# Linear attention and a top-1 expert layer on one core: PSUM banks apart, casts moved, key turns left out, late tiles routed singly, 112 partitions

## The chip, the core and the metric

The kernel runs on one core of a Trainium2 chip. A core has five engines with queues of their own: TensorE (PE, with its weight loads as PEld) multiplies matrices into PSUM, VectorE (DVE), ScalarE (ACT) and GpSimd (POOL) work on elements, and SyncE (SP) issues most transfers. Each queue runs in order; engines wait for each other by semaphores. The kernel uses PSUM as eight banks of 512 float32 values per partition. The metric is the device time in microseconds: 324.94 us before (median of three runs, 324.41 to 328.82).

## The reference

```python
for t in range(S):                                  # q, k, v, alpha: (B 4, H 8, S 768, D 48), float32
    state = alpha[:, :, t, :, None] * state + np.einsum('bhd,bhe->bhde', k[:, :, t], v[:, :, t])
    y[:, :, t] = np.einsum('bhd,bhde->bhe', q[:, :, t], state)
x = y.transpose(0, 2, 1, 3).reshape(3072, 384)
do = x @ w_skip > 0                                 # rows not chosen stay as they are
logits = x[do] @ w_gate                             # 8 experts
e_idx = argmax(logits); gate = softmax(logits)[e_idx]
out[do] = x[do] + gate * (relu(x[do] @ w1[e_idx]) @ w2[e_idx])    # w1: 384x1024, w2: 1024x384 per expert
```

## The kernel before

**Attention.** The 3072 rows are 24 tiles of 128 time steps (`NT`), all eight heads of one batch each; `G` = 2 batches alternate, six chunks (`C`) each. On partitions, keys, queries and decays (one buffer `qka`, loaded in three transfers) hold two heads of 48 features in rows 0 to 47 and 64 to 111; four such pairs (`NP`) lie side by side. Rows 48 to 63 and 112 to 127 are zeros. Per tile: two scans with the decays (`pfx`, `sfx`, L232, L240) and the products that scale queries and keys (L236, L242), three tiles ahead; scores into `ps_s` (L257), masked into `st` by VectorE (L266) and ScalarE (L272); the turned keys `kt` (`turn_k`, L280, L282) for the state update (`outer`, L293); the outputs into `ps_y` in two halves (L313). Between the halves `fence` makes ScalarE write one element, `spot` (L344), because both halves write the same bank. Then `turn_y`, and `rows` (L359) with the logits of the router.

**Routing.** `route` finds each row's expert (`m`), `rank` counts rows per expert with two matmuls, `place` makes slot numbers, `one_hot` and `marks` (`mv`) build the table that says which rows expert e gathers (L458). The steps of a group are handed out between the attention steps by `tick`. Tiles 18 to 23 come last; their rows for expert 0 are not fetched from memory but multiplied straight into place (`late_rows`, with the one-hot `mine`), and expert 0's other rows are fetched early (`early_rows`).

**Experts.** For each expert, four first-layer sets `up` of 18 products (L629) fill a bank of `ps_h` with two 240-column halves; ScalarE evicts `hh` (L633) and VectorE the rest `hl` (L634). Two second-layer passes `down` of 24 products (L645) follow; between them `turn` transposes the next expert's gathered rows in two halves through `ps_x` (L609, evicted at L611, L612). Weights are split into a high part on ScalarE and a low part on VectorE or GpSimd (L556, L560), a few pieces after each set. `guard` reads all decays and checks their range on ScalarE (`over`, L597) in experts 0 to 4. Both kinds of bank come from attention's tiles:

```python
self.ps = pp.tile([P, 2, 512], F32, name="ps_s")          # two banks, one tile
self.py = pp.tile([P, 2, 512], F32, name="ps_y")
self.ps_x = bank((self.ps[:, 0, :], self.ps[:, 1, :]), DM)
self.ps_h = bank((self.py[:, 0, :], self.py[:, 1, :], self.pg), 2 * ROOM)
```

The order on each engine is that of the program text; waits are put in by the framework, which follows PSUM accesses by tile.

## Time and profile before

| | |
|---|---|
| median of three runs | 324.94 us |
| the profiled execution: time, span | 327.61 us, 325.9 us |
| PE, PEld busy | 270.8 us (83%), 250.9 us (77%) |
| DVE, ACT, POOL busy | 198.2 us (61%), 159.5 us (49%), 179.2 us (55%) |
| transfers | 65.30 MB, mean 200 GB/s |
| attention, from the first scores to the last tile's rows | 7.8 to 136 us |
| experts, from the first set to the last pass | 143.9 to 319.3 us |

The span runs from the first to the last instruction; 1.7 us lie outside it. Busy shares are means over stages with different limits, so a change in one stage has to be read in that stage: which wait ends last there, and what then comes next. [...]

### The profile page before, as it was taken

The page shows a single profiled execution, that of the slowest core. Times are in us where ns is not written, and L with a number is a line of the kernel's source. Part 1 is how long each engine was busy: PE and PEld are TensorE (multiplying, and loading weights), DVE is VectorE, ACT ScalarE, POOL GpSimd, SP SyncE. Part 2 cuts the span into 40 slices and gives each one's busy share as a digit, 9 for nine tenths or more (in the row PEclk, how much of TensorE's full clock was granted, in tenths as well). Part 3 has the DMA queues.
Part 4 walks back from the last instruction along what each step waited for, and adds up shares of the span by engine and source line. Part 5 has one row for each costly group of instructions (what it writes and reads, how often), then busy time and mean ns, then how long its engine had stood idle before and what let it go on. Part 6 is the DMA issues. An engine that isn't in the chain of part 4 may idle for free.

```text
span 325.9 us, 9204 instructions
## 1 busy us (share of the span) xinstructions
PE 270.8 (83%) x3766; PEld 250.9 (77%) x3766; DVE 198.2 (61%) x362; ACT 159.5 (49%) x338; POOL 179.2 (55%) x199
## 2 busy tenths in 40 slices
PE   0798999898889799893989886878897888898891
PEld 0687987787778688683989886878887888898791
DVE  5765788778778886574555534535438456563720
ACT  3144554545456545612447385495495554453500
POOL 4545564648778978761574552643736265542611
PEclk9998999889999979996799997997999999999998
DMA  7987688969888964713372539449259557250001
GB/s 255 353 309 227 189 271 294 299 209 330 286 250 258 318 202 148 246 54 109 114 251 70 211 90 392 144 162 394 84 186 350 193 171 251 65 195 26 10 12 34
DMA packets 32178, 65.30 MB, mean 200 GB/s; under 512 B 4469, under 2 KB 11535, under 8 KB 32128
## 3 DMA queue, kind: packets, MB, share of 16 engines
q1 hardware_dynamic: 29952, 59.59, 54.9%
q0 software_dynamic: 2176, 5.05, 4.8%
q8 instruction: 31, 0.51, 0.6%
q14 instruction: 19, 0.16, 0.2%
HBM read 56.99 MB, written 8.85 MB: 202 GB/s over the span
## 4 chain that ended last, share of the span: by engine, by line
PE 59%; DVE 13%; ACT 8%; POOL 7%; issue 7%; DMA 3%; SPq 1%; POOLq 0%; DVEq 0%; ACTq 0%
PE ps_y L629 12%; PE ps_c L645 10%; PE ps_y L313 7%; PE ps_v L645 6%; PE ps_g L629 5%; PE ps_s L257 5%; PE ps_g L359 3%; PE ps_k L280 3%; ACT over L597 3%; DVE sfx L240 2%; PE ps_v L458 2%; PE ps_v L293 2%; ACT w1h L556 2%; PE ps_s L609 2%; DVE hl L634 2%
## 5 line engine op out<-in xcount | busy, mean ns | idle before, releaser
L257 PE MATMUL ps_s<-qka 64*64 64x128 f32 (+1 forms) x768 | 33.5, 270 | 11.1 <-DVE qka L242 7.8
L313 PE MATMUL ps_y<-st,vt 64*48 64x128 f32 (+1 forms) x768 | 36.7, 260 | 6.6 <-ACT spot L344 6.1
L560 POOL TENSOR_TENSOR w1l<-raw,w1h 128x512 fp32r<-128x512 f32 x24 | 31.3, 1305 | 17.0 <-ACT w1h L556 13.5
L629 PE MATMUL ps_y<-xh,w1h 128*128 128x240 f32 x132 | 25.3, 300 | 17.1 <-DVE hl L634 16.8
L242 POOL TENSOR_TENSOR qka<-qka,sfx 128x512 f32<-128x512 f32 x23 | 29.4, 1279 | 17.6 <-DVE sfx L240 12.8
L236 POOL TENSOR_TENSOR qka<-qka,pfx 128x512 f32<-128x512 f32 x24 | 26.3, 1095 | 21.1 <-DVE pfx L232 7.9
L651 POOL DMA_INDIRECT out_dram<-o,ids x16 | 17.6, 1098 | 36.9 <-DVE o L649 31.7
L257 PEld LDWEIGHTS ps_s<-qka 64*64 64x64 f32 x768 | 27.0, 143 | 12.4 <-POOL st L160 7.8
L560 POOL TENSOR_TENSOR w2l<-raw,w2h 128x512 fp32r<-128x512 f32 x16 | 21.2, 1327 | 27.1 <-ACT w2h L556 25.9
L629 PEld LDWEIGHTS ps_y<-xh,w1h 128*128 128x128 f32 x132 | 20.4, 205 | 18.8 <-DVE hl L634 18.4
L313 PEld LDWEIGHTS ps_y<-st,vt 64*48 64x48 f32 x768 | 26.8, 129 | 8.9 <-ACT spot L344 7.1
L272 ACT COPY st<-ps_s 64x512 f32<-64x512 f32 x24 | 13.9, 579 | 36.8 <-DVE st L266 30.4
L633 ACT ACTIVATE hh<-ps_y 128x480 fp32r<-128x480 f32 x22 | 12.5, 570 | 38.9 <-PE ps_y L629 35.7
L634 DVE SCALAR_TENSOR_TENSOR hl<-ps_y,hh 128x480 fp32r<-128x480 f32 x22 | 14.4, 652 | 28.1 <-ACT hh L633 28.1
L560 DVE TENSOR_TENSOR w2l<-raw,w2h 128x512 fp32r<-128x512 f32 x32 | 29.3, 935 | 2.8 <-ACT w2h L556 2.2
L232 DVE TENSOR_TENSOR_SCAN pfx<-qka,ps_c 128x527 f32<-128x527 f32 x24 | 29.6, 1233 | 2.2 <-DMA qka<-in_qka_dram 2.2
L240 DVE TENSOR_TENSOR_SCAN sfx<-qka,ps_c 128x525 f32<-128x525 f32 x24 | 29.7, 1238 | 0.3
L266 DVE COPY_PREDICATED st<-mask,ps_s 128x512 f32<-128x512 uint8 x24 | 17.5, 731 | 17.7 <-PE ps_s L257 16.2
L478 POOL DMA_INDIRECT xr<-out_dram,ids x18 | 20.0, 1110 | 13.4 <-DVE gates L495 7.7
L556 ACT CAST w1h<-raw 128x512 fp32r<-128x512 f32 x48 | 27.3, 619 | 0.0
L556 ACT CAST w2h<-raw 128x512 fp32r<-128x512 f32 x48 | 27.1, 616 | 0.0
L629 PE MATMUL ps_y<-xh,w1l 128*128 128x240 f32 x132 | 24.3, 293 | 0.0
(143 smaller groups left out, 711.8 us busy)
## 6 DMA issues: line engine op xcount, KB each, us to landing
raw<-in_w_dram SPq DMA_DIRECT2D x64, 384.0 KB, 5.0
qka<-in_qka_dram SPq DMA_DIRECT2D x48, 256.0 KB, 4.5
qka<-in_qka_dram SPq DMA_DIRECT2D x24, 263.5 KB, 4.2
vt<-in_v_dram SPq DMA_DIRECT2D x24, 192.0 KB, 4.6
out_dram<-x SPq DMA_DIRECT2D x24, 192.0 KB, 4.3
alpha<-in_nat_dram SPq DMA_DIRECT2D x8, 576.0 KB, 4.6
out_dram<-xr SPq DMA_DIRECT2D x6, 192.0 KB, 5.0
xr<-out_dram,ids POOLq DMA_INDIRECT x18, 3.5
```

Of the source, the lines that this page charges most:

```text
L232: nc.vector.tensor_tensor_scan(pfx[:, 0:DEC], dec, self.floor.to_broadcast([P, DEC]), FLOOR, ALU.mult, ALU.max)
L236: nc.gpsimd.tensor_tensor(w["qh"], w["qh"], pfx.rearrange("p (a w) -> p a w", w=SEG)[:, :, 1:P + 1], ALU.mult)
L240: nc.vector.tensor_tensor_scan(sfx[:, 2:DEC][:, ::-1], dec[:, 2:DEC][:, ::-1], self.floor.to_broadcast([P, DEC - 2]), FLOOR, ALU.mult, ALU ...
L242: (eng or nc.gpsimd).tensor_tensor(w["kh"], w["kh"], sfx.rearrange("p (a w) -> p a w", w=SEG)[:, :, 2:P + 2], ALU.mult)
L257: ins = self.nc.tensor.matmul(self.ps[t, r, o:o + (HP if s else P)], lhsT=kh[a, p, t], rhs=qh[a, p, s * HP:], start=True, stop=True, skip_ ...
L313: return self.nc.tensor.matmul(self.py[HP * c:HP * c + D, p % 2, o:o + n], lhsT=lhsT, rhs=rhs, start=first, stop=True, skip_group_check=True)
L478: return [self.nc.gpsimd.indirect_dma_start(out=xr[:n, j, :], out_offset=None, in_=self.out[:, :], in_offset=bass.IndirectOffsetOnAxis(ap= ...
L556: nc.scalar.copy(out=hi[:, s], in_=raw[:, s])
L560: eng.tensor_tensor(lo[:, s], raw[:, s], hi[:, s].bitcast(F32), ALU.subtract)
L629: nc.tensor.matmul(ps[:, u, :], lhsT=a[:, k, f * P:(f + 1) * P], rhs=b[:, k, :], start=(n == 0), stop=(n == len(order) - 1), skip_group_ch ...
L634: nc.vector.scalar_tensor_tensor(out=hl, in0=ps, scalar=0.0, in1=hh.bitcast(F32), op0=ALU.max, op1=ALU.subtract)
L645: nc.tensor.matmul(ps[:r], lhsT=a[:, f, js], rhs=b[:, f, :], start=(n == 0), stop=(n == 3 * FT - 1), skip_group_check=True)
```

## The change

Six edits. (1) In the expert stage, `ps_x` and `ps_h` get one tile per bank; attention's two-bank tiles move to pools that end with attention. (2) The casts of `tri` and `one_b` run one tile later on ScalarE, and the two steps that write `vals` run on VectorE instead of ScalarE and GpSimd. (3) `turn_k` is left out for the last chunk of a batch, whose turned keys nobody reads (4 of 24 tiles). (4) Tiles 18 to 23 are routed as groups of 3, 1, 1 and 1 instead of 4 and 2; their `mine`, `one_hot` and `marks` are made on VectorE, and the gates of all six in one pass. (5) The early fetch is issued after the split of tile 21. (6) Loads, scans, products and copies of keys, queries and decays use 112 partitions (`PD`).

```diff
 def banks(self, st):
-        self.ps = pp.tile([P, 2, 512], F32, name="ps_s")
-        self.py = pp.tile([P, 2, 512], F32, name="ps_y")
 def attention_pools(self, st):
+        both = lambda name: st.enter_context(tc.tile_pool(name=name, bufs=1, space=PSUM))
+        self.ps = both("ps_b").tile([P, 2, 512], F32, name="ps_s")
+        self.py = both("ps_d").tile([P, 2, 512], F32, name="ps_y")
 def expert_pools(self, st):
-        self.ps_x = bank((self.ps[:, 0, :], self.ps[:, 1, :]), DM)
-        self.ps_h = bank((self.py[:, 0, :], self.py[:, 1, :], self.pg), 2 * ROOM)
+        px = st.enter_context(tc.tile_pool(name="ps_x", bufs=1, space=PSUM))
+        ph = st.enter_context(tc.tile_pool(name="ps_h", bufs=1, space=PSUM))
+        self.ps_x = bank([px.tile([P, 512], F32, name=f"ps_x{n}") for n in range(2)], DM)
+        self.ps_h = bank([ph.tile([P, 512], F32, name=f"ps_h{n}") for n in range(2)] + [self.pg], 2 * ROOM)
 def rank_constants(self):
-        nc.scalar.copy(out=self.tri, in_=tri_f)
-        nc.scalar.copy(out=self.one_b, in_=self.ones)
+        self.rank_casts = [(self.tri, tri_f), (self.one_b, self.ones)]      # copied on ScalarE after tile 2
 def load(self, i, part=None, behind=None):
-            ins = nc.sync.dma_start(out=self.qkab[i % NQ][:, s], in_=self.qka[i, :, s])
+            ins = nc.sync.dma_start(out=self.qkab[i % NQ][:PD, s], in_=self.qka[i, :PD, s])
 def turn_k(self, i):
-        if i >= NT:
+        if i >= NT or self.chunk(i) == C - 1:
...
-        pk = self.pk.rearrange("p (a r) -> p a r", r=P)
+        pk = self.pk[:, 0:NP * PD].rearrange("p (a r) -> p a r", r=PD)
 def route(self, g, late=False):
-        nc.scalar.copy(out=self.vals[:, g0:g1, 2:3], in_=self.gate[:, g0:g1, :])
-        nc.gpsimd.tensor_tensor(self.vals[:, g0:g1, 3:4], self.gate[:, g0:g1, :],
-                                self.vals[:, g0:g1, 2:3].bitcast(F32), ALU.subtract)
+        if not late:
+            yield from self.gating(g, mx)
+    def route_one(self, i):
+        L = self.logit[:, i, 0:E]
+        nc.vector.tensor_reduce(out=mx, in_=L, op=ALU.max, axis=AX.X)
+        nc.vector.tensor_scalar(out=sk, in0=self.logit[:, i, E:E + 1], scalar1=0.0, scalar2=None, op0=ALU.is_gt)
+        nc.vector.scalar_tensor_tensor(out=e1, in0=L, scalar=mx, in1=self.rev[:, 0, :], op0=ALU.is_equal, op1=ALU.mult)
+        nc.vector.tensor_reduce(out=m2, in_=e1, op=ALU.max, axis=AX.X)
+        nc.vector.scalar_tensor_tensor(out=self.m[:, i, :], in0=e1, scalar=m2, in1=sk.to_broadcast([P, E]),
+                                       op0=ALU.is_equal, op1=ALU.mult)
+    def gating(self, g, mx):
+        yield nc.vector.tensor_tensor(d, self.logit[:, g0:g1, 0:E], mx.to_broadcast([P, n, E]), ALU.subtract)
+        yield nc.scalar.activation(out=ex, in_=d, func=AF.Exp)
...
+        yield nc.vector.tensor_copy(self.vals[:, g0:g1, 2:3], self.gate[:, g0:g1, :])
+        yield nc.vector.tensor_tensor(self.vals[:, g0:g1, 3:4], self.gate[:, g0:g1, :],
+                                      self.vals[:, g0:g1, 2:3].bitcast(F32), ALU.subtract)
 def static_path(self, ctx):                                                # after the last tile
-            for t in range(*groups[3]):
-                self.mine(t, nc.gpsimd)
...
+            self.rank(g21)
+            self.late_rows(18, range(KT))
+            put(g21)
+            self.mine(21, nc.vector)
+            self.route_one(22)
...
+            self.late_rows(19, range(KT))
+            self.rows(b)
+            self.logits(b)
+            self.row_copy(b)
+            self.rank(g22, [(self.one_b, self.cnt[:, 22, :]), (self.tri, self.m[:, 22, :])])
+            self.rank(g23, [(self.one_b, self.cnt[:, 22, :]), (self.one_b, self.m[:, 22, :])])
+            self.route_one(b)
+            put(g22)
+            self.mine(a, nc.vector)
+            self.late_split(b, nc.vector)
+            for t in (20, 21):
+                self.late_rows(t, range(KT))
+            self.rank(g23, [(self.tri, self.m[:, b, :])])
+            put(g23)
+            self.mine(b, nc.vector)
             self.early_turn()
             for t in (a, b):
                 self.late_rows(t, range(KT))
+            gates = self.gating((LATE, NT), self.lmx)
+            advance(gates, 2)
...
             self.first_turn()
+            advance(gates, 99)
+            self.marks((LATE, NT))
```

How this moves the order is shown at three places, with the waits in brackets (the engine whose semaphore is waited for; DMASW is a transfer issued by GpSimd).

TensorE, the turn for expert 3 between the two second-layer passes of expert 2, before:

```order
L645 MATMUL ps_c<-w2h,hl 128x384
L609 MATMUL ps_s<-ident,xr_2501 128x128 [waits DMASW2_49]
L609 MATMUL ps_s<-ident,xr_2501 128x128 x2
L609 MATMUL ps_s<-ident,xr_2501 128x112 [waits DMASW3_49,DVE_49]
L609 MATMUL ps_s<-ident,xr_2501 128x112 x2
L645 MATMUL ps_v<-w2h,hh 112x384
```

and with the change (`ps_x_2506` and `ps_x_2507` are the two banks):

```order
L675 MATMUL ps_c<-w2h,hl 128x384
L639 MATMUL ps_x_2506<-ident,xr_2510 128x128 [waits DMASW2_49]
L639 MATMUL ps_x_2506<-ident,xr_2510 128x128 x2
L639 MATMUL ps_x_2507<-ident,xr_2510 128x112 [waits DMASW3_49]
L639 MATMUL ps_x_2507<-ident,xr_2510 128x112 x2
L675 MATMUL ps_v<-w2h,hh 112x384
```

The second half no longer waits for VectorE, which evicts the first half.

TensorE, from the first to the second first-layer set of expert 3, before:

```order
L629 MATMUL ps_y<-xl,w1h 128x240 x3
L629 MATMUL ps_y<-xh,w1h 128x240 x3
L629 MATMUL ps_y<-xh,w1l 128x240 x3
L629 MATMUL ps_y<-xl,w1h 128x240 x3
L629 MATMUL ps_y<-xh,w1h 128x240 [waits DVE_49]
```

and with the change (`ps_h_2508` and `ps_h_2509` are two banks, the third is `ps_g` as before):

```order
L659 MATMUL ps_h_2508<-xl,w1h 128x240 x3
L659 MATMUL ps_h_2508<-xh,w1h 128x240 x3
L659 MATMUL ps_h_2508<-xh,w1l 128x240 x3
L659 MATMUL ps_h_2508<-xl,w1h 128x240 x3
L659 MATMUL ps_h_2509<-xh,w1h 128x240 x3
```

The second set starts without a wait for the first one's eviction.

ScalarE, around the `vals` cast of the first routing group, before:

```order
L365 COPY x<-ps_g 128x384 [waits DMAHW4_49,PE_49]
L282 COPY kt<-ps_k 128x512 [waits PE_49]
L410 CAST vals<-gate 128x6 [waits DVE_49]
L344 COPY spot<-ident 1x1 [waits PE_49,Activation_49]
L305 COPY state_104<-ps_v 128x192
```

and with the change:

```order
L366 COPY x<-ps_g 128x384 [waits DMAHW4_49,PE_49]
L283 COPY kt<-ps_k 128x448 [waits PE_49]
L345 COPY spot<-ident 1x1 [waits PE_49,Activation_49]
L306 COPY state_110<-ps_v 112x192 [waits DVE_49]
L273 COPY st_108<-ps_s 64x8x64 [waits DVE_49]
```

Between the copy of the turned keys and `spot` nothing waits for VectorE any more; the cast stands on VectorE's queue, behind the reciprocal and ahead of the masked copy `st`.

## Rows read from the trace of the kernel before

**Rows 1.** Windows: us, busy per engine (instructions), TensorE's granted clock, DMA share, GB/s.
```profile
15.00:120.00 105.00, 95.59 (x2282) 83.69 (x2278) 80.63 (x161) 52.01 (x131) 70.17 (x93) 0.95 0.86 271
173.00:319.30 146.30, 125.62 (x879) 121.92 (x877) 75.24 (x107) 80.38 (x148) 69.08 (x56) 0.98 0.48 168
```
**Rows 2.** Groups by line, TensorE: busy us, mean ns | idle before, released by.
```profile
L629 PE MATMUL ps_y<-xh,w1h 128*128 128x240 f32 x132 | 25.3, 300 | 17.1 <-DVE hl L634 16.8 <-ACT xh L523 0.2
```
**Rows 3.** Timeline of TensorE, experts 5 to 7: start, us, instruction [idle before, released by].
```profile
276.13 0.51 PE L609 MATMUL ps_s<-ident,xr 112*128 112x112 f32 x3 [1.16 <-DVE xl L612]
...
284.21 0.60 PE L629 MATMUL ps_y<-xh,w1h 128*128 128x240 f32 x3 [1.35 <-DVE hl L634]
...
296.24 0.51 PE L609 MATMUL ps_s<-ident,xr 112*128 112x112 f32 x3 [1.16 <-DVE xl L612]
```
**Rows 4.** Chain that ended last, experts: start, us, engine, tile, line, instructions merged.
```profile
148.39 2.37 PE ps_v L458 x12
...
153.91 4.20 PE ps_y L629 x18
...
199.70 3.90 PE ps_y L629 x18
203.60 2.02 PE ps_g L629 x18
205.62 4.20 PE ps_c L645 x24
...
220.82 3.75 PE ps_y L629 x18
...
284.21 2.29 PE ps_y L629 x18
```
**Rows 5.** Timeline of ScalarE, expert 2 to 3.
```profile
211.85 0.44 ACT L611 CAST xh<-ps_s 128x336 fp32r<-128x336 f32 x1 [1.19 <-PE ps_s L609]
...
219.53 0.55 ACT L633 ACTIVATE hh<-ps_y 128x480 fp32r<-128x480 f32 x1
219.98 1.12 ACT L556 CAST w2h<-raw 128x512 fp32r<-128x512 f32 x2
```
**Rows 6.** Timelines of TensorE and VectorE, from attention into expert 0.
```profile
137.43 0.38 PE L509 MATMUL ps_s<-mine,lateh 128*128 128x240 f32 x1 [0.99 <-POOL mine L440]
...
148.39 2.35 PE L458 MATMUL ps_v<-mv,hot 128*128 128x32 f32 x12 [2.21 <-POOL mv L450]
...
151.03 2.31 DVE L575 MEMSET xr<- 128x768 f32 x3 [3.56 <-PE ps_v L458]
...
153.91 1.00 PE L629 MATMUL ps_y<-xh,w1h 128*128 128x240 f32 x3 [3.16 <-DVE hl L634]
```
**Rows 7.** Timelines of TensorE and ScalarE, stalls in attention.
```profile
27.75 0.66 PE L313 MATMUL ps_y<-st,vt 64*48 64x64 f32 x16 [1.52 <-ACT spot L344]
...
61.94 0.20 ACT L410 CAST vals<-gate 128x6 fp32r<-128x6 f32 x1 [2.52 <-DVE gate L409]
...
62.27 0.65 PE L313 MATMUL ps_y<-st,vt 64*48 64x64 f32 x16 [1.60 <-ACT spot L344]
...
92.71 0.66 PE L313 MATMUL ps_y<-st,vt 64*48 64x64 f32 x16 [1.24 <-ACT spot L344]
```
**Rows 8.** Chain that ended last, attention: key turns and outputs after a stall, and later.
```profile
29.92 1.05 PE ps_k L280 x4
...
30.96 1.62 PE ps_y L313 x25
...
35.52 0.59 PE ps_k L280 x4
...
45.05 0.91 PE ps_y L313 x26
```
**Rows 9.** Transfers by line: KB each, us to landing.
```profile
qka<-in_qka_dram SPq DMA_DIRECT2D x48, 256.0 KB, 4.5
qka<-in_qka_dram SPq DMA_DIRECT2D x24, 263.5 KB, 4.2
```

More of the change, by code (lines that the diff above doesn't have):

```diff
@@ L182, in rank_constants @@
         self.gate = const.tile([P, NT, 1], F32, name="gate")
+        self.lmx = const.tile([P, NT - LATE, 1], F32, name="lmx")
     def slot_constants(self):
@@ L230, in decay @@
         if part == 0:
-            pfx = self.sc.tile([P, DEC + 1], F32, name="pfx", bufs=6)
-            nc.vector.tensor_tensor_scan(pfx[:, 0:DEC], dec, self.floor.to_broadcast([P, DEC]), FLOOR, ALU.mult,
+            pfx = self.sc.tile([P, DEC + 1], F32, name="pfx", bufs=6)[:PD]
+            nc.vector.tensor_tensor_scan(pfx[:, 0:DEC], dec, self.floor[:PD].to_broadcast([PD, DEC]), FLOOR, ALU.mult,
                                          ALU.max)
@@ L253, in scores @@
                 for r in range(2):
-                    a = slice(HP * r, HP * (r + 1))
+                    a = slice(HP * r, PD if r else HP)
                     t = slice(HP * s, HP * (s + 1))
@@ L382, in clear_late, with route @@
         self.nc.sync.dma_start(out=self.out[row:row + P, :], in_=self.xr0[:, 0, :])
-    def route(self, g, adder=None):
+    def route(self, g, late=False):
         nc = self.nc
@@ L392, in route @@
         bc = lambda a: a.to_broadcast([P, n, E])
-        mx, d, ex, m2, s1, eq = t1("mx"), t("d"), t("ex"), t1("m2"), t1("s1"), t("eq")
+        mx = self.lmx[:, g0 - LATE:g1 - LATE, :] if late else t1("mx")
+        m2, eq = t1("m2"), t("eq")
         e0, e1 = (a[:, :n, :] for a in self.p6[:2])
@@ L426, in place @@
         n = g1 - g0
-        pr = self.pv[:, TR:TR + n * E].rearrange("p (n e) -> p n e", e=E)
-        sl = self.sm.tile([P, GT, E], F32, name="sl")[:, :n, :]
-        s2 = self.late.tile([P, GT, 1], F32, name=f"s{g0}")[:, :n, :]
+        pr = self.ranks(g)
+        sl = self.late.tile([P, n, E], F32, name=f"sl{g0}")
+        s2 = self.late.tile([P, n, 1], F32, name=f"s{g0}")
         for i in range(g0, g1):
@@ L923, in static_path @@
                     self.table_add(first=True)
+                if i == 21:
+                    for _ in self.route(groups[3], True):
+                        pass
                 if i == 22:
+                    self.rank(groups[3])
                     self.table_add()
-                    self.early_rows()
-                    early = self.route(groups[3], nc.vector)
-                    advance(early, 7)
+                    ids = self.numbers(self.tab[:, :, 0:1, :], "ids0", 1)
+                    self.route_one(21)
+                    for _ in self.place(groups[3]):
+                        pass
+                    for t in range(18, 21):
+                        self.mine(t, nc.vector)
                 tick({18: 9}.get(i, 2))
@@ L935, in static_path @@
                     self.rank_constants()
+                if i == 2:
+                    for out, src in self.rank_casts:
+                        nc.scalar.copy(out=out, in_=src)
                 if i == 3:
@@ L940, in static_path, with put @@
             self.x0begun = set()
-            self.rank(groups[3])
-            for _ in self.place(groups[3]):
-                pass
-            for t in range(*groups[3]):
-                self.mine(t, nc.gpsimd)
+            g21, g22, g23 = groups[4:]
+            placed = {}
+            def put(g):
+                placed[g] = self.place(g)
+                next(placed[g])
+            self.rank(g21)
[3 more added lines that the diff above has]
+            self.route_one(22)
+            nc.vector.tensor_tensor(self.cnt[:, 22, :], self.cnt[:, 21, :], self.m[:, 21, :], ALU.add)
+            self.late_split(22)
+            self.late_rows(19, range(KT))
             self.rows(b)
@@ L948, in static_path @@
             self.row_copy(b)
-            last = self.route(groups[4], nc.vector)
-            advance(last, 7)
-            self.late_split(a)
+            self.rank(g22, [(self.one_b, self.cnt[:, 22, :]), (self.tri, self.m[:, 22, :])])
[3 more added lines that the diff above has]
+            self.mine(a, nc.vector)
             self.late_split(b, nc.vector)
-            self.late_rows(18, range(KT))
-            self.rank(groups[4])
-            for t in (19, 20):
+            for t in (20, 21):
                 self.late_rows(t, range(KT))
-            for n, _ in enumerate(self.place(groups[4])):
-                if n == 0:
-                    for t in (a, b):
-                        self.mine(t, nc.vector)
-            self.late_rows(21, range(KT))
+            self.rank(g23, [(self.tri, self.m[:, b, :])])
+            put(g23)
+            self.mine(b, nc.vector)
             self.early_turn()
@@ L964, in static_path @@
                 self.late_rows(t, range(KT))
-            self.first_turn()
-            for t in range(18, NT):
-                self.one_hot(t, nc.gpsimd if t % 2 else nc.vector)
-            advance(early, 99)
-            advance(last, 99)
-            for g in groups[3:]:
-                self.marks(g)
+            for g in groups[4:]:
+                advance(placed[g])
+            gates = self.gating((LATE, NT), self.lmx)
+            advance(gates, 2)
+            for t in range(18, 21):
+                self.one_hot(t, nc.vector)
+            self.first_turn()
+            advance(gates, 99)
+            self.marks((LATE, NT))
+            for t in range(21, NT):
+                self.one_hot(t, nc.vector)
+            for t in (a, b):
+                nc.vector.tensor_tensor(self.cnt[:, t + 1, :], self.cnt[:, t, :], self.m[:, t, :], ALU.add)
             self.store(a)
```

63 lines of the change are left out of this document (37 added, 26 removed).

## The prediction, made before the changed kernel was run

> **What bounds the kernel now.** I cut the span into stages with the busy times by window [rows 1]. From 15 to 120 us, the steady attention, TensorE is busy 95.6 of 105 us, VectorE 80.6 us and the DMA engines 86%. In the expert stage from 173 to 319.3 us TensorE is busy 125.6 of 146.3 us and nothing else comes near: VectorE 75, ScalarE 80, GpSimd 69 us, the DMA engines 48%. So the end of both stages is set by TensorE's own work plus what makes it wait, and the question for each edit is which of those waits it takes away and what is late next.
>
> The groups by line name the largest wait [rows 2]: TensorE stood 17.1 us before the first-layer products, 16.8 of it for `hl`, VectorE's eviction. The timeline shows the pattern [rows 3]: it waits before the second half of each turn of the gathered rows (1.16 us, once for each of experts 1 to 7) and about once per expert before a first-layer set. These are waits for the neighbouring bank: `ps_x` has two banks and `ps_h` three, but two of each are halves of one tile, and the order rows of the change part show a VectorE wait exactly where a set in one half follows a set in the other. [...]
>
> **Term A, banks apart, experts 1 to 7.** In the new order neither wait is there: a set in one half of `ps_h` waits only for the eviction of its own bank, three sets earlier. Removed: 16.8 − 3.16 = 13.6 us before first-layer sets (the 3.16 are expert 0's, below); 7 × 1.16 = 8.1 at the turns; (3.90 − 2.02) + (3.75 − 2.02) = 3.6 of slow clock; five restarts at 0.27 = 1.4. Together 26.7. Check: from the turn at 276.13 to the one at 296.24 are 20.11 us [rows 3]; less 1.16, 1.35 and 0.27 it is 17.3, which is four sets at 2.02, two second-layer passes at 4.20 [rows 4] and 0.8 for the turn: TensorE alone.
>
> What is late next? In experts 1 to 4 ScalarE also runs the range check (`over`), and its queue is the cover to look at [rows 5]. It begins `xh` at 211.85, as TensorE ends the turn, and is busy without a gap until `hh` of the next expert's first set starts at 219.53, 7.7 us later. TensorE ends that set after 4.2 + 2.0 us, so `hh` is 1.5 us late, as before; but with three free banks that stops nobody, since the first bank is wanted again only after 4.2 + 3 × 2.0 = 10.3 us. After that ScalarE does one `hh` and a pair of casts per set (0.55 and 1.12 us, less with their overlap, against 2.02 of products) and catches up before the next second layer needs the last pieces of `w2`. I take the whole 26.7. Bounds: I know nothing that makes it more; if `w2` ends up to 2 us late in each of the four experts with the check, it is 18.7.
>
> **Term B, the way into the experts** [rows 6]. Expert 0's second set waited 3.16 us for `hl`, because VectorE first cleared three gather buffers (from 151.03, released by the table products). That is a bank wait too and goes; now the fourth set is the first to need `hl`, two sets later. That second set then took 4.20 us, and the table products before it 2.37 [rows 4], both at the low clock; at the high one they are 2.02 and about half of 2.37, so 2.2 + 1.2 us are to be had if the clock holds. It fell around the 2.21 us that the table waited for `mv`. That path gets shorter: one gating pass for six tiles instead of two, with the two `vals` steps and the marks on VectorE, so no hop to ScalarE and GpSimd and back; some short VectorE operations and three one-hots remain. I take half of the 2.21 away. Late tiles singly: TensorE waited 0.99 us for GpSimd's first `mine`, which is now made one tile earlier, on VectorE, with the products spread between the routing steps: 0.8. The early fetch moves on GpSimd's queue behind the split of tile 21; its rows are wanted only after the products of four late tiles, which cover it. Sum 8.4, taken as 8. Bounds: 3.2 (the bank wait alone, the clock stays low) and 10 (the table doesn't wait at all).
>
> **Term C, attention** [rows 7]. Three TensorE stalls before the second half of `ps_y` end with ScalarE's `spot`: 1.52, 1.60 and 1.24 us. In the second ScalarE stood at its `vals` cast at 61.94, which had waited 2.52 us for VectorE's gate, with `spot` queued behind it; the third is the same, and the first is the cast of `tri`, whose input GpSimd had only just made. All three casts leave that place. A stall of this kind near 113 us stays, since there `ex` still waits for `d` ahead of `spot`. After the first the clock fell as well [rows 8]: a key turn took 1.05 instead of 0.59 us, the next `ps_y` 1.62 instead of 0.91, that is 1.2 us; for the second I estimate 0.8 by it. Four key turns, each 0.59 us of products, go (2.4), and the 20 others have 112 instead of 128 moving columns: 20 × 0.59 / 8 = 1.5 us if time goes by columns. All in all 10.3. What may take it back: VectorE is busy 77% there and gets two more short `vals` steps per group; queued behind them is the masked copy `st`, which TensorE wants only in the next tile's first half, after rows, outer product and key turn, and that work is their cover. I take 7.5. Bounds: 3 (VectorE stops TensorE almost wherever ScalarE did) and 10.3.
>
> **The narrower loads and work.** Scans, products and copies have as many elements per partition as before, so I cost them at nothing. The loads carry 12.5% fewer rows [rows 9]: of 48 × 256 + 24 × 263.5 KB = 18.6 MB, 2.3 MB less. No stall of the steady attention ends with a load, so I put 0 on it; the bad side is a rival below.
>
> **Sum.** 26.7 + 8 + 7.5 = 42.2 us. The profiled execution has a span of 325.9 us and took 327.61, so it would come to 283.7 and 285.4. It stands 2.7 us above the median of the runs, 324.94; taken from the median the forecast is **283 us**. All upper bounds together save 47 (278 us), all lower ones 25 (300 us).
>
> **Rivals.**
> *ScalarE takes the place of the banks.* In the four experts with the check the `w2` pieces end late and TensorE stands 2 us in each. For it: 7.7 us of unbroken queue [rows 5]. Against it: 80 us of ScalarE work in 146 us. Saving 34, time 291 us. Chance 0.15.
> *VectorE takes the place of ScalarE* in attention and at the way in. The steps taken from ScalarE and GpSimd land on an engine busy 77%, and the clock still falls at the table. B is 3.2 and C 3: saving 33, time 292 us. Chance 0.12.
> *The 112-row loads cost more than the 128-row ones: slower.* Transfers keep the DMA engines busy 90 of the 105 us [rows 1], for 28.5 MB. The keys, queries and decays of 18 of the 24 tiles fall there (six are loaded before): 14 MB, half, so 44 us, and 46 for the rest. Term C shrinks the stage to 97, so the loads bind once one costs 1.15 times what it does now. Slower by over 2% needs the stage to grow by 41 us (35 of A and B and 6.5 of margin): a factor of 2.3. At 2.5 the stage takes 156 us and the kernel 341. Against it: if a load's price goes by rows, the engines are busy 85 us instead of 90, well under 97, and 112 rows still divide evenly among 16 engines; no row of the trace has such a load. Chance 0.03.
> [...]
> *The bank change does nothing*, because something else still ties the banks: only C and the rest of B come, about 312 us. The order of waits speaks against it. Chance 0.02.
>
> **How the numbers follow.** The forecast, 277 to 289 us, has 0.68; the first two rivals 0.27, around 291; the others 0.05. The range 277 to 299 us takes in the forecast, both near rivals and nearly all of the lower bounds: my 8 in 10. Differences within 2% (6.5 us) count as no change, about what a measurement of this kernel can tell. Faster 0.95, within 2% 0.02, slower 0.03.
>
> **What would show it.** In the new profile: before first-layer products no wait for VectorE, and turns of six products in one piece; 17.3 to 17.6 us per expert in experts 1 to 7; no stall before `ps_y` at the places of the first three, one left near `ex`; the table products within 1.5 us of the end of the first set, at full clock. Wrong would be: TensorE waiting for `w2l` or `hh` in experts 1 to 4 (first rival), for `st` or `mine` (second), or scans waiting for `qka` loads with the DMA engines over 95% busy (third).

## The result

The changed kernel takes 296.8 us (median of four runs, 294.0 to 299.5) against 326.1 us (four runs, 324.4 to 328.8): ratio 0.907, 95% interval 0.896 to 0.917. Ratios leave out executions that lay well above the fastest of their kernel; medians count all. The direction and the largest term were forecast rightly; against 283 us it is 14 us too long. The profiled execution has a span of 295.0 us: 30.9 us were saved, 42.2 forecast. The page after:

```profile
span 295.0 us, 9180 instructions
PE 260.2 (88%) x3755; PEld 244.3 (83%) x3755; DVE 206.2 (70%) x385; ACT 154.6 (52%) x328; POOL 173.1 (59%) x185
PEclk9999999999999995985979999999999999999997
```

The two stages as windows, with the columns of [rows 1]; the expert stage ends earlier, so its window is another:

```profile
15.00:120.00 105.00, 91.80 (x2310) 81.04 (x2302) 85.72 (x170) 51.09 (x129) 72.17 (x92) 0.97 0.89 259
167.00:288.50 121.50, 119.71 (x880) 118.67 (x878) 80.20 (x111) 79.34 (x148) 72.67 (x58) 1.00 0.58 205
```

In the expert stage TensorE is now busy 119.7 of 121.5 us at a granted clock of 1.00 (a share of full speed, as in every window). In attention it is busy 91.8 of 105 us, less than the 95.6 of [rows 1], and idle 13.2 instead of 9.4. The span of the profiles, cut at four marks of TensorE's timeline:

| stretch | before, us | after, us | forecast saving | saving |
|---|---|---|---|---|
| start to the end of the last scores | 129.7 | 127.3 | 7.5 | 2.4 |
| from there to the first first-layer set | 14.2 | 18.3 | 0.8 | −4.2 |
| from there to the table products | 4.5 | 2.7 | 1.1 | 1.8 |
| from there to the last product | 170.9 | 139.9 | 33.3 | 31.0 |

(33.3 is term A with the 3.16, 2.2 and 1.2 us of B.) The experts gave 2.3 us less than forecast, attention and the late tiles together 10. The chain that ended last shows the expert stage:

```profile
148.38 1.75 PE ps_v L487 x12
...
249.89 0.62 PE ps_x L639 x6
250.51 4.19 PE ps_v L675 x24
254.70 4.05 PE ps_h L659 x36
258.75 2.03 PE ps_g L659 x18
...
267.00 0.62 PE ps_x L639 x6
```

Two sets follow each other without a step (4.05 us for 36 products), the turn is one piece of 0.62 us where [rows 3] had a wait of 1.16 inside it, and from this turn to the next it takes 17.1 us. The group that lost 17.1 us in [rows 2] loses 0.2 for `xh`, and its neighbour one wait of another engine, 1.52 us at 169.30 in expert 1:

```profile
L659 PE MATMUL ps_h<-xh,w1l 128*128 128x240 f32 x132 | 23.0, 279 | 1.5 <-POOL w1l L588 1.5
L659 PE MATMUL ps_h<-xh,w1h 128*128 128x240 f32 x132 | 22.9, 279 | 0.2 <-ACT xh L551 0.2
```

In attention the three `spot` stalls of [rows 7] are gone, one is left near `ex` at 109.71, as forecast. These are now TensorE's waits of 0.6 us and more in the timeline, from 15 us on to the late tiles. (`xt` is ScalarE's copy of the outputs out of `ps_y`, made by `turn_y` and read by `rows`; `hot` is what `one_hot` makes on GpSimd; `issue` stands where the profile shows nothing that was waited for.)

```profile
28.95 0.32 PE L314 MATMUL ps_y<-qka,state 48*48 48x128 f32 x3 [2.11 <-issue]
35.38 0.42 PE L314 MATMUL ps_y<-st,vt 64*48 64x128 f32 x9 [1.74 <-issue]
55.85 0.65 PE L314 MATMUL ps_y<-st,vt 64*48 64x64 f32 x15 [1.76 <-issue]
62.80 0.66 PE L314 MATMUL ps_y<-qka,state 64*48 64x128 f32 x16 [0.63 <-ACT xt L352]
67.01 0.66 PE L314 MATMUL ps_y<-qka,state 64*48 64x128 f32 x16 [0.94 <-ACT xt L352]
71.25 0.40 PE L487 MATMUL ps_v<-mv,hot 128*128 128x32 f32 x2 [0.97 <-POOL hot L474]
90.59 0.39 PE L487 MATMUL ps_v<-mv,hot 128*128 128x32 f32 x2 [1.00 <-POOL hot L474]
96.25 0.40 PE L487 MATMUL ps_v<-mv,hot 128*128 128x32 f32 x2 [1.09 <-POOL hot L474]
109.71 0.72 PE L314 MATMUL ps_y<-st,vt 64*48 64x64 f32 x16 [1.74 <-ACT spot L345]
131.90 1.11 PE L314 MATMUL ps_y<-qka,state 64*48 64x128 f32 x16 [1.73 <-ACT xt L352]
```

For the stalls removed there are new ones: `xt`, `hot` (the wait of 0.97 us stood there before too, at 74.52), and places that end with nothing shown. The 16 products at 131.90 take 1.11 us; the same 16 of the tile ahead took 0.66 at 125.37. The granted clock is 0.50 over the first and 1.00 over the second; from 131.9 to 141 us it is 0.51, and 1.00 from there to the table products. The stretch from the last scores to the first set, as a window with the columns of [rows 1], before and after:

```profile
129.73:143.90 14.17, 12.40 (x168) 10.62 (x161) 8.79 (x36) 5.41 (x13) 12.04 (x13) 1.00 0.53 172
```

```profile
127.33:145.65 18.32, 15.80 (x167) 13.67 (x162) 11.27 (x52) 5.26 (x13) 5.12 (x5) 0.72 0.38 132
```

Of the 4.2 us lost there, TensorE is busy for 3.4, at a granted clock of 0.72 instead of 1.00, and idle for 0.8.

### The profile page after: what moved, and what is told of

The parts are those of the page before. It is cut to its first block, busy times and chain, and to the rows that moved or that the text cites. A ratio compares the mean times of both kernels' runs of the same rounds, so it can differ in the third digit from the quotient of the medians.

```text
span 295.0 us, 9180 instructions
## 1 busy us (share of the span) xinstructions
PE 260.2 (88%) x3755; PEld 244.3 (83%) x3755; DVE 206.2 (70%) x385; ACT 154.6 (52%) x328; POOL 173.1 (59%) x185
## 4 chain that ended last, share of the span: by engine, by line
PE 70%; DVE 10%; POOL 7%; issue 5%; DMA 3%; ACT 2%; SPq 1%; POOLq 0%
PE ps_h L659 15%; PE ps_c L675 10%; PE ps_v L675 10%; PE ps_y L314 8%; PE ps_g L659 7%; PE ps_s L258 5%; PE ps_g L360 5%; DVE sfx L241 3%; PE ps_k L281 2%; PE ps_v L294 2%; DMA qka<-in_qka_dram 2%; DVE st L267 2%; POOL hot L474 2%; POOL xr L507 1%; PE ps_v L487 1%
## 5 line engine op out<-in xcount | busy, mean ns | idle before, releaser
L258 PE MATMUL ps_s<-qka 64*64 64x128 f32 (+3 forms) x768 | 32.3, 267 | 9.6 <-DVE qka L243 7.8
L243 POOL TENSOR_TENSOR qka<-qka,sfx 112x512 f32<-112x512 f32 x23 | 29.6, 1286 | 18.1 <-DVE sfx L241 11.3
L237 POOL TENSOR_TENSOR qka<-qka,pfx 112x512 f32<-112x512 f32 x24 | 26.2, 1092 | 20.7 <-DVE pfx L233 7.8
L258 PEld LDWEIGHTS ps_s<-qka 48*64 48x64 f32 (+1 forms) x768 | 26.2, 142 | 10.5 <-POOL st L161 7.8
L507 POOL DMA_INDIRECT xr<-out_dram,ids x18 | 21.0, 1167 | 21.3 <-DMA alpha<-in_nat_dram 17.1
L233 DVE TENSOR_TENSOR_SCAN pfx<-qka,ps_c 112x527 f32<-112x527 f32 x24 | 29.6, 1233 | 2.2 <-DMA qka<-in_qka_dram 2.2
L241 DVE TENSOR_TENSOR_SCAN sfx<-qka,ps_c 112x525 f32<-112x525 f32 x24 | 29.7, 1239 | 0.3
L267 DVE COPY_PREDICATED st<-mask,ps_s 128x512 f32<-128x512 uint8 x24 | 17.6, 735 | 12.2 <-PE ps_s L258 10.6
L588 DVE TENSOR_TENSOR w1l<-raw,w1h 128x512 fp32r<-128x512 f32 x24 | 23.3, 980 | 2.6 <-ACT w1h L584 2.5
L360 PE MATMUL ps_g<-xw,xt 112*64 112x105 f32 x384 | 24.9, 276 | 0.0
L659 PE MATMUL ps_h<-xh,w1l 128*128 128x240 f32 x132 | 23.0, 279 | 1.5 <-POOL w1l L588 1.5
L659 PE MATMUL ps_h<-xh,w1h 128*128 128x240 f32 x132 | 22.9, 279 | 0.2 <-ACT xh L551 0.2
```

The source lines that it names most:

```text
L233: nc.vector.tensor_tensor_scan(pfx[:, 0:DEC], dec, self.floor[:PD].to_broadcast([PD, DEC]), FLOOR, ALU.mult, ALU.max)
L237: nc.gpsimd.tensor_tensor(w["qh"], w["qh"], pfx.rearrange("p (a w) -> p a w", w=SEG)[:, :, 1:P + 1], ALU.mult)
L241: nc.vector.tensor_tensor_scan(sfx[:, 2:DEC][:, ::-1], dec[:, 2:DEC][:, ::-1], self.floor[:PD].to_broadcast([PD, DEC - 2]), FLOOR, ALU.mul ...
L243: (eng or nc.gpsimd).tensor_tensor(w["kh"], w["kh"], sfx.rearrange("p (a w) -> p a w", w=SEG)[:, :, 2:P + 2], ALU.mult)
L258: ins = self.nc.tensor.matmul(self.ps[t, r, o:o + (HP if s else P)], lhsT=kh[a, p, t], rhs=qh[a, p, s * HP:], start=True, stop=True, skip_ ...
L360: ins = self.nc.tensor.matmul(self.pg[t, p * RW:(p + 1) * RW], lhsT=w["xt"][:PD, p, t], rhs=self.xw[:PD, p, :], start=True, stop=True, ski ...
```

## The experiments

All ratios are to the kernel before, run beside them on the same chip, with their 95% intervals; the runs come from several chips, so kernels of different chips are compared by ratio. "Last scores" is the end of the last score product in the profile.

**The banks alone, and everything but the banks.**

```diff
-        self.ps_x = bank((self.ps[:, 0, :], self.ps[:, 1, :]), DM)
+        self.ps_x = bank([px.tile([P, 512], F32, name=f"ps_x{n}") for n in range(2)], DM)
```

(and the same for `ps_h` and attention's pools; the second kernel has it the other way round.)

> The kernel before with edit (1) alone. Theory: the whole saving of the change came after the table products (30.9 of 30.9 us of span), so it comes from the banks; this kernel is then as fast as the full change, time ratio 0.90 to 0.91, turns 17.1 us apart in experts 2 to 7, no wait of TensorE before first-layer products for hl, and the first first-layer set still at 143.9 us. Rival: the expert stage also gained from what came ahead of it (the shorter gating, GpSimd freed of marks and one-hots); then this kernel saves 27 us or less, ratio 0.92 or above, with a wait left in expert 0.

> The changed kernel with edit (1) taken back: both halves of each bank pair in one tile again. Theory: edits (2) to (6) bring nothing that lasts, so this kernel stands within 1% of the kernel before, 323 to 330 us, with the waits for hl and xl back in the experts (25 to 28 us). Rival, the prediction's terms C and the rest of B: 7.5 + 2.7 us are there once the banks don't mask them, and the time is 315 to 319 us.

> The kernel before with edit (1) alone once more, on the same chip as the two beside it: 290 to 294 us, ratio to before 0.89 to 0.90, as in its first run; it is what both are to be compared with. If it comes above 295, its first run was a lucky one and the other five edits are worth something after all.

> The changed kernel once more, beside the three below on one chip, for what the first profile of it owed to where the clock fell. Theory: the other five edits cost about what they bring, so it stands 0.5 to 2% behind the kernel before with edit (1) alone (291.0 us in its run, 296.8 here in the first); ratio to before 0.895 to 0.91, and TensorE's idle time with nothing shown in the attention is again 3 to 6.5 us. Rival: the first profile was an unlucky one; then it comes to 291 us or less.

Measured: the banks alone 291.0 us, 0.894 (0.886 to 0.902), and again 293.2 us, 0.908 (0.902 to 0.914); all but the banks 329.0 us, 0.993 (0.987 to 0.999); the change again 297.9 us, 0.898 (0.889 to 0.906), with five executions of 292.8 to 298.4 us and one of 854.6, as the kernel before had one of 886.8 beside it. With the banks alone TensorE needs 138.9 us from the table products to the last one, and the turns are 17.1 apart; without them the wait is back:

```profile
L656 PE MATMUL ps_y<-xh,w1h 128*128 128x240 f32 x132 | 25.2, 300 | 17.1 <-DVE hl L661 16.9 <-ACT xh L550 0.2
```

So edit (1) carries the result. The five others are worth 0.1 to 1.3% without the banks, and on top of the banks no gain is shown: the change's 0.907 and 0.898 stand beside 0.894 and 0.908. With the banks alone the first set starts at 138.2 us, not at the 143.9 expected, since attention took 5.7 us less with the instructions of before. In its second profile the change idled only 1.0 us with nothing shown, not the 3 to 6.5 expected, so these places vary from one execution to the next; its last scores ended at 129.7 even so (granted clock from 15 to 120 us 0.93, in the first 0.97).

**The banks and the casts.** Edit (1) with edit (2) on top of it, the closest test of term C (shown in part; the second `vals` step moves from GpSimd to VectorE as well):

```diff
-        nc.scalar.copy(out=self.vals[:, g0:g1, 2:3], in_=self.gate[:, g0:g1, :])
+        yield nc.vector.tensor_copy(self.vals[:, g0:g1, 2:3], self.gate[:, g0:g1, :])
...
+                if i == 2:
+                    for out, src in self.rank_casts:
+                        nc.scalar.copy(out=out, in_=src)
```

> The kernel before with edits (1) and (2): the banks, and the casts of tri, one_b and vals off their place on ScalarE. Loads and work stay on 128 partitions, the key turns stay. Theory (term C's first part): three of the four stalls that end with spot (7.0 us in four with the banks alone) go and nothing takes their place, the last scores end 3 to 5 us earlier than the 124.05 us with the banks alone, the time is 1 to 1.7% below it. Rival: GpSimd, busy 19.5 of 23 us there, is late with hot instead, and VectorE with st; waits for hot and xt rise by 2 us or more, and the time stays within 0.7% of it.

Measured: 294.6 us, 0.901 (0.895 to 0.906); last scores at 124.03, with the banks alone at 124.05. TensorE's waits in the timeline with the banks alone,

```profile
26.02 0.66 PE L314 MATMUL ps_y<-st,vt 64*48 64x64 f32 x16 [2.04 <-ACT spot L345]
58.96 0.65 PE L314 MATMUL ps_y<-st,vt 64*48 64x64 f32 x16 [1.25 <-ACT spot L345]
69.68 0.40 PE L459 MATMUL ps_v<-mv,hot 128*128 128x32 f32 x2 [0.97 <-POOL hot L446]
87.53 0.65 PE L314 MATMUL ps_y<-st,vt 64*48 64x64 f32 x16 [1.99 <-ACT spot L345]
94.31 0.40 PE L459 MATMUL ps_v<-mv,hot 128*128 128x32 f32 x2 [0.27 <-POOL hot L446]
107.89 0.66 PE L314 MATMUL ps_y<-st,vt 64*48 64x64 f32 x16 [1.76 <-ACT spot L345]
```

and with the casts moved as well:

```profile
32.71 0.43 PE L313 MATMUL ps_y<-st,vt 64*48 64x128 f32 x9 [1.38 <-issue]
47.93 0.44 PE L257 MATMUL ps_s<-qka 64*64 64x64 f32 x9 [1.35 <-issue]
61.12 0.66 PE L313 MATMUL ps_y<-qka,state 64*48 64x128 f32 x16 [1.88 <-ACT xt L351]
69.56 0.40 PE L458 MATMUL ps_v<-mv,hot 128*128 128x32 f32 x2 [0.97 <-POOL hot L445]
88.74 0.40 PE L458 MATMUL ps_v<-mv,hot 128*128 128x32 f32 x2 [1.25 <-POOL hot L445]
94.39 0.40 PE L458 MATMUL ps_v<-mv,hot 128*128 128x32 f32 x2 [1.06 <-POOL hot L445]
107.97 0.66 PE L313 MATMUL ps_y<-st,vt 64*48 64x64 f32 x16 [1.76 <-ACT spot L344]
```

The same products start at 69.6, 94.3 and 107.9 in both: 5.3 us of `spot` stalls are gone, and 2.2 (`xt`), 1.9 (`hot`) and 2.5 us (nothing shown) have come (two waits of the first tiles are 1.2 us shorter). The second profile of the banks alone, which idled 2.5 us with nothing shown too, had 5.9 us of `spot` stalls and 2.4 of waits for `hot`, and its last scores ended at 123.96, so the pair's match isn't owed to those idle places. The rival held; in time, 0.901 lies between the two ratios of the banks alone.

Why `xt` waits is seen in the changed kernel at 59 us; VectorE, GpSimd and ScalarE, from its timelines:

```profile
59.54 0.17 DVE L433 RECIPROCAL gate<-s 128x6 f32<-128x6 f32 x1
59.74 1.27 DVE L434 CAST vals<-gate 128x6 fp32r<-128x6 f32 x1
60.92 0.73 DVE L267 COPY_PREDICATED st<-mask,ps_s 128x512 f32<-128x512 uint8 x1
```

```profile
59.71 1.27 POOL L243 TENSOR_TENSOR qka<-qka,sfx 112x512 f32<-112x512 f32 x1 [1.42 <-DVE gate L433]
```

```profile
61.69 0.58 ACT L273 COPY st<-ps_s 64x512 f32<-64x512 f32 x1 [1.78 <-DVE vals L435]
62.17 0.58 ACT L352 COPY xt<-ps_y 112x512 f32<-112x512 f32 x1
```

The cast of six values per partition takes 1.27 us on VectorE, not the 0.2 that it took on ScalarE [rows 7]. GpSimd's product, released by the same `gate`, starts 0.03 us ahead of it and lasts exactly as long. So it is again at 88.40 (1.27 us beside 1.28, with a start 0.04 us later); the two casts of this line at 113.81 and 147.56, with GpSimd idle, take 0.16 and 0.17 us. The masked `st`, ScalarE's half of `st` and `xt` then stand in line behind it (ScalarE starts at 61.69, as the masked `st` ends; the profile names `vals` L435, the instruction behind it). What keeps the cast that long is not shown.

**The loads.** 128 rows in the changed kernel, the work on 112:

```diff
-            ins = nc.sync.dma_start(out=self.qkab[i % NQ][:PD, s], in_=self.qka[i, :PD, s])
+            ins = nc.sync.dma_start(out=self.qkab[i % NQ][:, s], in_=self.qka[i, :, s])
```

The other way, on the kernel with the banks alone:

```diff
-            ins = nc.sync.dma_start(out=self.qkab[i % NQ][:, s], in_=self.qka[i, :, s])
+            n = P if i < NQ else PD
+            ins = nc.sync.dma_start(out=self.qkab[i % NQ][:n, s], in_=self.qka[i, :n, s])
```

> The changed kernel, but the loads of keys, queries and decays move 128 rows again; the work stays on 112. Theory: the 112-row loads keep the DMA engines busy longer than the 128-row ones (packet of 2048 bytes 119 ns on the mean against 104 before), and TensorE's instruction blocks come late behind them: the idle time of TensorE that ends with nothing shown, 6.4 us in five places of the attention, falls to 1.6 us or less as before the change; the last scores come 3 to 5 us earlier and the time is 1 to 1.5% below that of the change. Rival: the idle places come because attention runs faster and uses up instructions sooner, whatever is loaded; then they stay at 5 us or more, and the larger loads change the time by less than 1 us or make it longer.

> The kernel before with edit (1), and with 112 instead of 128 rows loaded for keys, queries and decays of tiles 6 to 23 (rows 112 to 127 keep the zeros that tiles 0 to 5 brought; all work stays on 128). Theory: the 112-row loads cost time; packets of 2048 bytes take 115 to 120 ns on the mean instead of 100, TensorE's idle time with nothing shown rises from 0.26 to 3 us or more, the last scores end 2.5 to 5 us later than 124.05 and the time is 0.8 to 1.7% above the banks alone. Rival: those idle places have nothing to do with the rows; then idle time, last scores and time stay within 1 us of the banks alone.

Measured: 293.2 us, 0.899 (0.892 to 0.906), idle time with nothing shown 2.6 us, last scores at 125.4; and, narrower loads on the banks alone, 297.1 us, 0.905 (0.900 to 0.910), idle 1.15 us, last scores at 123.0, 1.1 us earlier than without. The first lies between theory and rival. The second speaks against the theory of late scores: its idle time lies between the 0.3 and 2.5 us of the two profiles of the banks alone, and so does its ratio between theirs. A narrower load itself took longer from issue to landing here, 5.1 against 4.7 us; transfers of the changed kernel, then with 128 rows (KB each, us):

```profile
qka<-in_qka_dram SPq DMA_DIRECT2D x48, 224.0 KB, 5.1
```

```profile
qka<-in_qka_dram SPq DMA_DIRECT2D x48, 256.0 KB, 4.7
```

Each packet of 2048 bytes took 119 ns on the mean, against 104 before the change and 98 with 128 rows again; on the banks alone 110 with the narrower loads (115 to 120 expected) and 100 without. A cost in the kernel's time isn't shown, nor why the narrower load took longer.

**Keys and late routing.** The key turns of the last chunks put back:

```diff
-        if i >= NT or self.chunk(i) == C - 1:
+        if i >= NT:
```

and, in another kernel, the routing of tiles 18 to 20 moved:

```diff
                 self.causal(i + 1)
+                if i == 22:
+                    for _ in self.route(groups[3], True):
+                        pass
...
-                if i == 21:
-                    for _ in self.route(groups[3], True):
-                        pass
```

> The changed kernel with the four key turns of the last chunks put back (their copies on ScalarE too). Theory: they were the cover under which ScalarE finished xt, so leaving them out turned into waits for xt of 0.63, 0.94 and 1.73 us and, after the last, 9 us at the low clock; with them the first two waits are gone, the third is 0.7 us shorter, the clock holds after it or falls later, and the first first-layer set comes 0 to 4 us earlier; time 0 to 1.3% below that of the change. Rival: the turns cost what their products take, 4 x 0.59 us, and the waits come from VectorE; then the waits stay beside them, and the time is 0.5 to 0.8% above that of the change.

> The changed kernel with VectorE's routing steps of tiles 18 to 20 moved behind the masked copy st of tile 23. Theory (the prediction's second rival, at another place): nine routing steps and two one-hots stand ahead of st on VectorE, st starts at 130.0 instead of 127.4, xt is queued behind st's other half on ScalarE, TensorE waits 0.56 for cnt and 1.73 us for xt and falls to the low clock until 141.0. With the move both waits shrink to 0.5 us together, TensorE keeps the high clock there, and the first first-layer set comes 4 to 6 us earlier, at 140 to 142; time 1.3 to 2% below the change. Rival: the wait comes from the key turns that are no longer there as cover, and the routing only moves to a later wait before the late tiles' products: the first set comes less than 1.5 us earlier.

Measured: keys kept 295.2 us, 0.900 (0.891 to 0.909); a wait of 2.02 us for `xt` stays at 60.80, where the cast holds up VectorE, and one of 0.60 has come at 119.76, but the one of 1.73 us at the end is gone, and from the last scores to the first set it is 14.1 instead of 18.3 us. Routing later: 293.6 us, 0.899 (0.892 to 0.906); the wait for `xt` at the end is gone, one for `cnt` is 1.18 us, and the stretch takes 14.6 us. In time neither can be told from the change. With the routing later, `st` starts ahead of the routing steps, at 126.91, so `xt` is brought forward. With the keys kept the cover isn't the whole of it: a key turn is 0.6 us of products, and in that profile the granted clock was already lower over the last scores (0.81 from 124 to 128.75), so `xt` had more time. The stretch goes with the clock in all profiles: 14.0 to 14.6 us where it was 0.88 or more, 15.3 to 18.3 where it was 0.72 to 0.81. It took 17.2 and 17.4 us with the casts or the narrower loads on the banks alone, which have the key turns and the old routing, and 15.3 with 128-row loads and neither edit here; so the lower clock there does not hang on key turns and routing alone. What stood ahead of `st` there, on VectorE in the changed kernel:

```profile
125.75 2.58 DVE L474 TENSOR_SCALAR hot<-slots,s 128x256 fp32r<-128x256 f32 x2
128.26 0.17 DVE L397 TENSOR_REDUCE lmx<-ps_c 128x3 f32<-128x24 f32 x1
...
129.56 0.56 DVE L405 TENSOR_TENSOR cnt<-cnt,m 128x8 bf16<-128x8 bf16 x3
130.03 0.72 DVE L267 COPY_PREDICATED st<-mask,ps_s 128x512 f32<-128x512 uint8 x1
```

**Queue order.** `hot` is made ahead of GpSimd's products with the decays, and `xt` copied ahead of ScalarE's half of `st`:

```diff
                 self.causal(i + 1)
-                self.cross(i + 1)
...
                 tick(2)
+                if 10 <= i < 22:
+                    self.one_hot(i - 10, nc.gpsimd)
                 self.decay(i + 3, 0)
...
                 self.turn_y(i)
+                self.cross(i + 1)
...
-                if 10 <= i < 22:
-                    self.one_hot(i - 10, nc.gpsimd)
```

> The changed kernel with two steps of the attention moved in their queues: GpSimd makes the one-hot hot ahead of the products with the decays instead of behind them, and ScalarE copies xt ahead of its half of the next tile's st instead of behind it. Theory (queue order): the stalls that ended with spot came back as waits for hot (3.7 to 3.8 us in the changed kernel, 1.7 before) and xt (1.6 to 2.5 us, none before) because these two stand last on their queues; moved ahead, hot falls below 1 us and xt below 0.5, the last scores end 3 to 5 us earlier than 127.3 to 129.7, and the time is 1 to 1.5% below the change. Rival (amount of work): GpSimd is busy 19 of 20 to 23 us there and VectorE 18, so a wait for another of their results (st, qka) takes their place; TensorE's waits after the first two scores still sum to 12 us or more and the last scores end no earlier than 126.

Measured: 289.0 us, 0.887 (0.881 to 0.894); no wait for `hot`, one for `xt` of 0.72 us (below 0.5 expected), last scores at 123.3, in a profile of the longest of its six executions. The theory held in the main, though 5.7 us with nothing shown remained, 3.24 of them in one place; the ratio is clear of the change's 0.907, not of its 0.898 (0.889 to 0.906).

**Together.** These moves with the keys kept, the later routing, 128-row loads, and fewer routing steps in tile 18:

```diff
-                tick({18: 9}.get(i, 2))
+                tick({18: 6}.get(i, 2))
```

> The changed kernel with all that the runs so far point to: the two moves of the run beside it, the key turns kept, the routing steps of tiles 18 to 20 behind st of tile 23, 128-row loads, and six instead of nine routing steps in tile 18, so that the exponential ex is no longer ahead of spot there (1.75 us of stall and 6.8 us at the low clock in the changed kernel). Theory: the waits are each a matter of queue order, so the gains add: last scores at 119 to 122, first first-layer set 14 us later at 133 to 136, table after 2.7, end 139.5 later; time 278 to 283 us. Rival (amount of work, and a clock that falls elsewhere): last scores at 123 or later, time within 1% of the kernel with the banks alone.

Measured: 282.9 us, 0.872 (0.866 to 0.878), against 293.2 us for the banks alone on the same chip: faster than both kernels, and 3.5% below the banks alone. Which of the edits added to the two moves gave how much was not separated. Last scores end at 115.6, the first set starts at 129.65, and the only wait of TensorE over 1 us between the first tiles and the last scores is this one:

```profile
105.35 0.67 PE L294 MATMUL ps_v<-vt,kt 128*64 128x48 f32 x16 [1.20 <-ACT state L306]
```

TensorE is busy 91.9 of 95 us there:

```profile
15.00:110.00 95.00, 91.94 (x2375) 81.79 (x2370) 85.01 (x173) 53.77 (x136) 74.06 (x95) 0.98 0.93 303
```

and the long cast, still 1.27 us, stops nobody, because `xt` no longer stands behind it (VectorE, then ScalarE):

```profile
54.46 1.27 DVE L434 CAST vals<-gate 128x6 fp32r<-128x6 f32 x1
```

```profile
54.95 0.59 ACT L352 COPY xt<-ps_y 112x512 f32<-112x512 f32 x1 [1.19 <-PE ps_y L314]
56.40 0.58 ACT L273 COPY st<-ps_s 64x512 f32<-64x512 f32 x1 [0.86 <-DVE vals L435]
```

**The casts taken back from it.** Edit (2) undone in the combined kernel (shown in part), `vals` on ScalarE and GpSimd:

```diff
-        yield nc.vector.tensor_copy(self.vals[:, g0:g1, 2:3], self.gate[:, g0:g1, :])
+        nc.scalar.copy(out=self.vals[:, g0:g1, 2:3], in_=self.gate[:, g0:g1, :])
```

> The combined kernel (282.9 us, no spot stall) with edit (2) taken back: tri and one_b cast at once on ScalarE, the two vals steps on ScalarE and GpSimd. Theory (term C was right on the mechanism, and hidden by waits further back): now that hot and xt stand first in their queues, the casts cost what they were said to cost: two or three spot stalls of 1.2 to 2.0 us come back, 3.5 to 5.5 us with no other wait falling, the last scores end at 119 to 122 instead of 115.6, the table waits 0.5 to 1.5 us more for mv, and the time is 286 to 289 us. Rival: the moves alone took the slack out, and the casts are hidden again; last scores by 117, time below 285.

Measured: 281.8 us, 0.880 (0.873 to 0.886), on another chip, where the kernel before varied more (320.4 to 358.6 us). Three `spot` stalls (3.4 us together) are back in the profile, and its last scores come at 120.9, where the theory had them; but that execution took 287.4 us and the other six 281.1 to 283.7, so sizes aren't read from its trace. The time is the rival's, below 285; by the ratio, whose interval overlaps the combined kernel's (0.866 to 0.878), the two can't be told apart. That the casts are worth anything is not shown even here, and that they are worth nothing isn't either.

## Why the prediction was right in direction and 14 us too fast

296.8 us lies inside the range of 277 to 299 us, near its end, and outside the 277 to 289 that had 0.68. It is inside because term A, nearly two thirds of the sum, came almost whole. Term C came to 2.4 us, under its lower bound of 3, and term B, if A is taken whole, to 1.9, under its 3.2. The two rivals near 291 us, for which the range reached that far, are not what happened, so part of the hit is luck.

*Term A and the bank wait of term B* held. The order rows said that no wait would be left; 33.3 us were forecast from the table on, 31.0 came, 32.0 with the banks alone. (The slow sets and the restarts are those of [rows 4]: the granted clock before was 0.56 and 0.58 over the sets of 3.90 and 3.75 us, 1.00 over those of 2.02 and 2.29. Five restarts were counted where the trace has six, 0.3 us.) The expected 17.3 to 17.6 us per expert are 17.1 (17.4 once), except for 19.2 in expert 1. Part of the 2.3 us short is a wait there that was not foreseen, 1.52 us for GpSimd's `w1l` (0.9 to 2.5 us in every kernel with the banks apart). Another part is the clock: it was 1.00 from the table products to 151.0 us, but it fell behind them, to a mean of 0.53 from 151.0 to 154.6 us, where term B had put it high "if the clock holds". Its half of 2.37 us for the table products no run shows: at 1.00 they took 1.75 us here. The first rival, ScalarE late with `w2`, never came: no wait for `w2` or `hh` in any expert, as the reasoning on three free banks had it.

*Term C failed*, by the step "after rows, outer product and key turn, and that work is their cover", with "two more short `vals` steps". The three stalls went as said; their gain did not come. One of the two steps takes 1.27 us, as long as the GpSimd product that starts with it, and the cover ends in ScalarE's queue, where `xt` stood behind `st`. At the other places it was GpSimd that came late with `hot`. This comes nearest to the second rival, VectorE in ScalarE's place, with GpSimd beside it; it had 0.12. Its sign, waits for `st` or `mine`, did not show: TensorE waited for what stands behind `st`. It left C a saving of 3 us; measured are 2.4 in the change and 0 in the pair with and without the casts. Even the 2.4 are read against a long execution: with the banks alone attention has the instructions of before, and its last scores ended at 124.0 in both profiles, not 129.7; the granted clock from 15 to 120 us was 0.98 and 1.00 there and 0.95 in [rows 1].

*The key turns* were costed as 2.4 us saved. At the end they were part of the cover for `xt`: leaving them out, with the routing ahead of `st`, brought the wait of 1.73 us, and behind it the granted clock is 0.51 until 141 us. The 20 turns left start their next products 0.54 instead of 0.59 us later, 1.0 us in all (1.5 forecast). *Late tiles singly* were to give 0.8 us, and the stretch lost 4.2; the wait for `mine` is gone as said, but the term put the clock there at nothing, and TensorE was busy 3.4 us longer at 0.72 instead of 1.00. What edits (4) and (5) are worth by themselves was not measured. The shorter way to the table gave 1.8 us, forecast 1.1; it is 2.7 or 2.8 us from first set to table in every profile that routes singly.

*The narrower loads* at 0 stand: a transfer that takes longer, and no time shown. A load of the form that comes 48 times took 112 packets of 119 ns, 13.3 us of packet time, as the 128 of 104 ns did before (12.5 with the 98 ns of the run with 128 rows); the third rival needed 1.15 times as much. The scans wait 2.2 us for loads in all, as before. Third and fourth rivals did not occur.

So of the 42.2 us, 30.9 came: 5.1 were lost in attention, 5.0 between the last scores and the first set, 2.3 in the experts, 0.7 came back at the table, and 0.4 is rounding. That the combined kernel takes 282.9 us, the number forecast, is chance: it holds moves that the change does not.

## What to carry to other kernels

In this attention, with TensorE, VectorE and GpSimd busy 91.8, 85.7 and 72.2 of 105 us, taking one wait away moved the end only until the next queue was late. So follow what stands behind the moved step on its new engine, and what its result stands ahead of. A small copy put on VectorE cost here as much as the GpSimd instruction beside it, 1.27 us instead of 0.16, where the same result released both. The largest gain behind that of the banks came with moving results that TensorE waits for to the front of their queues (0.887, and 0.872 with four edits more); whether removed stalls count after that is not shown.

## What was not expected of the hardware

TensorE's idle places with nothing shown stand in the middle of runs of equal products, and their distances repeat. Between two of them in the changed kernel lie 127 products with 127 weight loads, as this window shows (columns as in [rows 1], the counts of PE and PEld in brackets):

```profile
49.47:55.84 6.37, 4.62 (x127) 4.00 (x127) 4.98 (x14) 3.10 (x8) 3.58 (x5) 1.00 0.99 270
```

Between others, here and in the other profiles, lie 254, 381, 508, 634 and 761, two to six times as many. The queue of instruction transfers moved 31 packets in 0.51 MB in the changed kernel, blocks of about 16 KB each, and the 3755 products of the page make 29.6 stretches of 127; so it is likely, as an estimate from these counts, that TensorE waits there for the next block of its program. It was not tested by itself. How long a block was in transfer (up to 1.73 us in the changed kernel's attention, 2.4 with the banks alone) doesn't tell which ones come late: with the banks alone these places cost 0.3 us, and 2.5 in the second profile. In all profiles they cost 0.3 to 6.4 us, and 6.4 and 1.0 in the two of the changed kernel, so that a single profile of attention is uncertain by some 5 us from them alone.
